# Attention with a spectral mixer on one core: instructions re-ordered within each engine by a table of moves

## The chip, the cores and the metric

One core of one Trainium2 chip runs the kernel: a matrix engine (TensorE, PE in the rows, its weight loads listed apart as PEld), VectorE (DVE), ScalarE (ACT), GpSimd (POOL), and SyncE (SP), whose queue issues nearly all transfers. The metric is device time in microseconds (us) of one launch. A profile of one execution gives the start, the length and the releasing event of each instruction.

## What is computed

Eight batches, each with eight heads of 576 positions and 64 channels. First attention with a threshold: of each score row only the entries within `tau` of the maximum are kept. Then a mixing layer over the 512 channels of a batch.

```
scores = (q @ k^T) / 8
scores = where(scores >= max(scores) - tau, scores, -1e9)
attn = exp(scores - max); attn = attn / (sum(attn) + 1e-9)
x = heads side by side of attn @ v             # per batch 576 x 512
theta = x @ w_theta
y = w_tok_r @ (x * cos(theta)) + w_tok_i @ (x * sin(theta))
u = x + y
out = u + max(u @ w_ch, 0)
```

## The kernel before

**Work.** Two heads make a pair; there are 32 pairs, four to a batch. A pair has five *units* of query rows, four with two heads of 128 rows and a last one in which both heads share 128 rows. Every fp32 operand of a product is split into a high and a low part (`xh` and `xl`, `q1` and `q2`, `k1` and `k2`), and three of the four cross products are taken.

**A unit.** Scores (L594: 12 matmuls of 288 columns, 6 in the last unit) go into the PSUM banks 0 to 3. VectorE reads each head's scores with its row maximum (L610) and so frees the banks; ScalarE takes the exponential (L635); VectorE masks and sums (L642). The weights are then turned round: in pairs 0 to 4 and in every fourth pair by TensorE (L675, copied out by ScalarE at L681 and L693), in the other 20 pairs by VectorE (L657, L659).

**A pair's end.** The product with v is L740 in the first kind of pair (72 matmuls in one run) and L711 in the second, where it works on 32-row by 64-column parts of the matrix engine; an L711 product comes in three blocks of 48 program matmuls (96 in the trace, since fp32 takes two passes), which the planner may place apart. The row sums are inverted by VectorE (L760, L764), transposed by TensorE (L768), sent through DRAM and multiplied into x by GpSimd (L791) or VectorE (L797).

**A batch's mixer.** Theta products and, at the end, w_ch products (both L843, 96 matmuls of 288 columns each), sines and cosines on ScalarE, transposes of z (L970) whose high and low parts are ScalarE's L976 and VectorE's L979, and 216 token matmuls (L999). The mixer of batch b runs between the pairs of batch b+1; the last batch's runs alone at the end. At the start the mixer's weights are split too (`convert`, L440 to L502).

**Order.** Nothing is ordered by hand. Every operation is recorded with a `key`, a due time built from the offsets in `AT`; `Plan.run` goes through a modelled execution, on each engine takes the ready operation with the lowest key, and then emits all instructions in order of their planned starts. Engines run their own lists in order and wait for each other by semaphores. PE's list is the one the rest hangs on. TensorE's instructions are counted in `supply`, in blocks of 256.

Of the kernel before, what the change touches and what calls it, by code (L numbers as in the profile page):

```python
# [10 lines left out]
F32 = mybir.dt.float32  # L11
# [18 lines left out]
BLOCK = 256  # L30
FETCH = 3.6
# [4 lines left out]
    "wait": 0.095, "margin": 46.124, "held": 12.206, "theta": 2.0, "theta_by": 8.31, "tok": 13.85, "tok_by": 3.19, "ch": 37.95,  # L36
    "ch_by": 9.28, "q": -2.78, "k": -4.2, "raw": 1.32, "v": 5.53, "m0": 8.11, "m1": 8.41, "score": -169.95, "nm": -1.15,
    "add": 0.82, "exp": -1.46, "mask": 2.68, "wrap": -18.89, "turn": 4.88, "copy": 2.04, "block": -0.74, "turn_by": -34.35,
    "last": 6.86, "v0": 2.89, "v1": 3.55, "vcopy": 9.91, "div": -3.88, "rows": 6.2, "dmul": 15.26, "x": -12.78, "x_by": 4.06,
# [3 lines left out]
    "n_rb": 2, "n_ang": 2, "n_xh": 4, "n_xl": 4, "n_wm": 3, "n_z": 3, "n_k": 4, "n_s2": 3, "n_nm": 4, "n_sc": 4, "n_a": 1,  # L43
    "n_zh4": 4, "n_zl4": 4, "n_zh1": 2, "n_zl1": 2, "n_xT": 7, "n_v": 1, "n_rows": 2, "n_rt": 1, "keep": -144.9,
    "linger": 0.174, "v_r": 1.74, "v_m": -2.19, "t_s": 1.07, "m_s": -9.19, "wc": 14, "early": 5, "each": 1, "ka": 4, "vq": 1,
    "pd": 3, "vs": 8.05, "parts": 3, "ab": 0, "sq": 2,
}

# [9 lines left out]
def BY_PE(n):  # L58
    return n < AT["early"] or n % 4 >= 4 - AT["each"]


def ON_POOL(what, n, j):
    if what == "q":
        return n >= 32 - AT["pq"]
    if what == "k":
        return j < AT["pk"]
    if what == "x":
        return j < AT["px"]
    if what == "u":
        return j < AT["pu"]  # L70
    return n < AT["pz"]
# [51 lines left out]
class Plan:  # L123
# [39 lines left out]
    def run(self):  # L163
        free = [0.7] * 5
        cand = [[] for _ in range(5)]
# [8 lines left out]
        block = [80, 0.0]  # L174

        def supply(o, t, occ):
            left, (at, ready), x = o.count, block, t
            while at + left >= BLOCK:
                x, left, at = max(x + (BLOCK - at) * occ / o.count, ready), left - BLOCK + at, 0
                ready = x + FETCH  # L180
            return x + left * occ / max(o.count, 1) - t - occ, [at + left, ready]
# [55 lines left out]
        while todo:  # L237
# [37 lines left out]
            for d in o.after:  # L275
                d.ready = max(d.ready, o.end + SEM if d.deps[o] else t)
# [5 lines left out]
        self.ops.sort(key=lambda o: (o.start, o.n))  # L282
        for o in self.ops:
            o.fn()
# [3 lines left out]
def tile_attn_moe(  # L288
# [36 lines left out]
    nc.sync.dma_start(tau_sb, tau.broadcast_to([P, 1]))  # L325
# [86 lines left out]
    wt_b = fixed(wt_h)  # L412

    def convert(src, n, raw_cls, places, key, done, turn):
# [125 lines left out]

    def prepare_q(n, key):
        pr = pairs[n]
        raw = sb("rawq", [P, QS])
        load(lambda: nc.sync.dma_start(raw(), qT[n // NP, n % NP]), key + AT["raw"], (), (raw,), 320)
        q1, q2 = pr.q = [sb("q", [P, QS], F32R) for _ in range(2)]
        if n >= AT["sq"]:
            act(
                c_act(QS, ptr=True), lambda: nc.scalar.activation(out=raw(), in_=raw(), func=AF.Copy, scale=gate), key,
                (raw,), (raw,),
            )  # L550
        act(c_act(QS), lambda: nc.scalar.copy(out=q1(), in_=raw()), key, (raw,), (q1,))
        low(ON_POOL("q", n, 0), lambda: q2(), lambda: raw(), lambda: q1().bitcast(F32), key, (raw, q1), (q2, 0), QS)

    def prepare_k(n, key):
        pr = pairs[n]
        raw = sb("rawk", [P, S])
        load(lambda: nc.sync.dma_start(raw(), kT[n // NP, n % NP]), key + AT["raw"], (), (raw,), 288)
        k1, k2 = pr.k = [sb("k", [P, S], F32R) for _ in range(2)]
        act(c_act(S), lambda: nc.scalar.copy(out=k1(), in_=raw()), key, (raw,), (k1,))  # L559
        low(ON_POOL("k", n, 0), lambda: k2(), lambda: raw(), lambda: k1().bitcast(F32), key, (raw, k1), (k2, 0))  # L560

    def load_v(n, key):
# [3 lines left out]

        def issue():
# [594 lines left out]
```

## Time and profile before

| | |
|---|---|
| time, three runs | 965.24, 966.85, 967.28 us; median 966.85 us |
| the profiled execution | 966.37 us, of which 964.6 us lie between its first and last instruction |
| PE busy | 914.9 us, 95% of the span |
| DVE, ACT, POOL busy | 816.2, 612.4, 353.4 us |
| granted TensorE clock | 1.00 (2.4 GHz) in every slice |

A busy PE is not PE at its peak: a matmul's end is modelled, about 0.3 us after its start, while the next one starts 0.13 us after it in a full run. A wait on PE therefore shows as idle time only beyond that.

### The profile page before, as it was taken

What the parts mean: (1) busy time and instruction counts of PE and PEld (TensorE: products, weight loads), DVE (VectorE), ACT (ScalarE), POOL (GpSimd) and SP (SyncE); (2) the same over time, 40 slices, a digit from 0 to 9 for tenths busy, and PEclk for the clock granted to TensorE, in tenths of its full rate; (3) what the DMA queues carried; (4) which work ended last, traced back from release to release, by engine and by line L of the source; (5) the groups of instructions that cost most, each with busy time, mean ns of one, the idle gap of its engine ahead of it and who ended that gap; (6) DMA issues with size and microseconds to landing.
All of it is one profiled execution on the core that took longest, in us unless ns stands there. A gap on an engine that the chain in (4) does not pass through costs nothing.

```text
span 964.6 us, 30108 instructions
## 1 busy us (share of the span) xinstructions
PE 914.9 (95%) x12532; PEld 804.4 (83%) x12532; DVE 816.2 (85%) x1981; ACT 612.4 (63%) x1156; POOL 353.4 (37%) x378
## 2 busy tenths in 40 slices
PE   5899899999999999999999999999999999999998
PEld 4567788897889889888898888888898878898898
DVE  6999989979899798879898798888898798985452
ACT  6889898447764667447874667637774467634550
POOL 4337635304362233522553242612443244510210
PEclk9999999999999999999999999999999999999999
DMA  7458244536613464325533365224633354123402
GB/s 236 124 157 252 64 126 140 144 120 188 176 53 83 127 188 119 90 65 162 182 79 96 99 201 142 69 61 143 187 98 90 100 170 150 47 56 106 158 8 72
DMA packets 60152, 118.81 MB, mean 123 GB/s; under 512 B 20560, under 2 KB 29296, under 8 KB 57456
## 3 DMA queue, kind: packets, MB, share of 16 engines
q1 hardware_dynamic: 60016, 116.90, 41.4%
q8 instruction: 98, 1.61, 0.7%
q14 instruction: 38, 0.31, 0.1%
HBM read 103.09 MB, written 13.78 MB: 121 GB/s over the span
## 4 chain that ended last, share of the span: by engine, by line
PE 52%; DVE 34%; ACT 7%; issue 4%; DMA 1%; POOL 1%; SPq 0%; DVEq 0%; ACTq 0%
PE banks_ps__66 L999 14%; PE banks_ps__66 L843 10%; PE banks_ps__66 L711 9%; DVE s L642 8%; DVE sc L610 8%; PE banks_ps__66 L594 8%; DVE a L657 6%; PE banks_ps__66 L675 4%; PE banks_ps__66 L740 3%; DVE zl L979 2%; DVE nm L619 1%; PE banks_ps__66 L970 1%; ACT s L635 1%; DVE z L895 1%; DVE xl L402 1%
## 5 line engine op out<-in xcount | busy, mean ns | idle before, releaser
L635 ACT ACTIVATE s<-sc,nm 128x576 f32<-128x576 f32 x288 | 218.2, 778 | 116.8 <-DVE sc L610 107.8
L642 DVE SCALAR_TENSOR_TENSOR s<-sc,nm,s 128x576 f32<-128x576 f32 x288 | 255.1, 900 | 7.2 <-ACT s L635 5.3
L610 DVE TENSOR_SCALAR_CACHE_REDUCE sc<-banks_ps__66 128x576 f32<-128x576 f32 x270 | 195.6, 739 | 18.1 <-PE banks_ps__66 L594 17.9
L594 PE MATMUL banks_ps__66<-k,q 64*128 64x288 f32 (+1 forms) x1728 | 176.8, 312 | 19.1 <-DVE sc L610 10.2
L594 PEld LDWEIGHTS banks_ps__66<-k,q 64*128 64x128 f32 (+1 forms) x1728 | 138.6, 188 | 48.1 <-DVE sc L610 19.5
L843 PE MATMUL banks_ps__66<-xh,wm 128*128 128x288 f32 x1024 | 173.2, 303 | 0.4 <-ACT xh L804 0.4
L999 PE MATMUL banks_ps__66<-wt_h,zh 128*128 128x288 f32 x576 | 159.5, 300 | 1.1 <-DVE zl L979 1.1
L999 PE MATMUL banks_ps__66<-wt_l,zh 128*128 128x288 f32 x576 | 159.8, 300 | 0.0
L843 PEld LDWEIGHTS banks_ps__66<-xh,wm 128*128 128x128 f32 x1024 | 143.8, 188 | 11.6 <-issue 9.2
L945 POOL TENSOR_TENSOR z<-z,xT 128x288 f32<-128x288 f32 x112 | 95.2, 886 | 143.3 <-ACT z L926 143.3
L657 DVE STREAM_TRANSPOSE a<-s 128x576 f32<-128x576 f32 x160 | 116.4, 756 | 14.5 <-PE banks_ps__66 L711 11.2
L791 POOL TENSOR_TENSOR xT<-xT,rb 128x288 f32<-128x288 f32 x48 | 38.4, 819 | 226.1 <-ACT xT L724 122.5
L711 PE MATMUL banks_ps__66<-a,v 32*64 32x144 f32 x5760 | 110.0, 287 | 5.5 <-issue 5.5
L999 PEld LDWEIGHTS banks_ps__66<-wt_h,zh 128*128 128x128 f32 x576 | 108.2, 188 | 4.4 <-issue 2.8
L999 PEld LDWEIGHTS banks_ps__66<-wt_l,zh 128*128 128x128 f32 x576 | 108.2, 188 | 4.0 <-issue 3.7
L711 PEld LDWEIGHTS banks_ps__66<-a,v 32*64 32x64 f32 x5760 | 91.8, 130 | 17.9 <-issue 17.1
L402 POOL TENSOR_TENSOR k<-rawk,k 128x288 fp32r<-128x288 f32 x64 | 64.7, 1031 | 107.2 <-ACT k L559 70.3
L999 PE MATMUL banks_ps__66<-wt_h,zl 128*128 128x288 f32 x576 | 96.0, 301 | 0.0
L843 PE MATMUL banks_ps__66<-xl,wm 128*128 128x288 f32 x512 | 94.5, 301 | 0.0
L402 POOL TENSOR_TENSOR xl<-xT,xh 128x288 fp32r<-128x288 f32 x64 | 62.5, 1003 | 71.5 <-ACT xh L804 70.1
L999 PEld LDWEIGHTS banks_ps__66<-wt_h,zl 128*128 128x128 f32 x576 | 81.0, 188 | 5.1 <-issue 5.0
L979 DVE TENSOR_TENSOR zl<-banks_ps__66,zh 128x512 fp32r<-128x512 f32 (+1 forms) x96 | 50.0, 544 | 34.0 <-ACT zh L976 33.3
(81 smaller groups left out, 1314.6 us busy)
## 6 DMA issues: line engine op xcount, KB each, us to landing
wm<-wm_dram SPq DMA_DIRECT2D x64, 512.0 KB
v<-in_vp_dram SPq DMA_DIRECT2D x104, 288.0 KB
rawq<-in_qT_dram SPq DMA_DIRECT2D x32, 320.0 KB
rawk<-in_kT_dram SPq DMA_DIRECT2D x32, 288.0 KB
out_dram<-xT SPq DMA_DIRECT2D x31, 288.0 KB
rb<-sums_dram SPq DMA_DIRECT2D x64, 128.0 KB
z<-in_w_tok_dram SPq DMA_DIRECT2D x9, 576.0 KB
wm_dram<-rb SPq DMA_DIRECT2D x16, 256.0 KB
```

The costliest lines, as they stand in the source:

```text
L402: eng.tensor_tensor(out=out()[:, c0:c1], in0=in0()[:, c0:c1], in1=in1()[:, c0:c1], op=ALU.subtract)
L594: nc.tensor.matmul(ps()[:, 2 * j + h, :HS], q[a]()[r, i * P : (i + 1) * P], k[c]()[r, h * HS : (h + 1) * HS], start=(x == 0), stop=(x == 2),)
L610: lambda j=j, sc=sc, scaled=scaled: nc.vector.tensor_scalar(out=sc().rearrange("p (a b) -> p a b", a=2), in0=ps()[:, 2 * j : 2 * j + 2, :H ...
L635: lambda j=j, sc=sc, weights=weights: nc.scalar.activation(out=weights(), in_=keys(sc()), func=AF.Exp, bias=nm()[:, j : j + 1], scale=-1.0),
L642: lambda j=j, sc=sc, total=total, weights=weights: nc.vector.scalar_tensor_tensor(out=weights(), in0=keys(sc()), scalar=nm()[:, 2 + j : 3 ...
L657: nc.vector.transpose(out=a()[:, :, j, 32 * i : 32 * i + 32], in_=src.rearrange("p (c q) -> p c q", q=32))
L675: nc.tensor.transpose(out=tp()[: k1 - k0, c * P : (c + 1) * P], in_=flat()[:, k0:k1], identity=ident)
L711: nc.tensor.matmul(ps()[64 * h : 64 * h + 64, b, :w], v()[r, c, h, :], a()[r, c, h, :], start=(c == 0), stop=(c == 17))
L843: nc.tensor.matmul(ps[h]()[:, :HS], wm()[:, a, c, :], parts[c][bb]()[:, h * HS : (h + 1) * HS], start=first and n == 0, stop=final and n = ...
L945: eng.tensor_tensor(out=zi, in0=zi, in1=x[m]()[:, c0:c1], op=ALU.mult)
L979: lambda zh=zh, zl=zl, tv=tv: nc.vector.tensor_tensor(out=zl(), in0=tv(), in1=zh().bitcast(F32), op=ALU.subtract),
L999: nc.tensor.matmul(ps()[:, :HS], zz[c][lo]()[:, zz[c][2]], w[:, c, hs], start=(q + n == 0), stop=(q + n == len(work) - 1),)
```

## The change

Five things are changed; the arithmetic of the result is the same, and each line issues as many matmuls as before.

1. The offsets in `AT` are new, with extra offsets for pairs 0 to 7 (`h_`) and from pair 28 on (`e_`); the planner adds a latency (`pad_`) to a dependence on another engine, and models TensorE's instruction blocks with a lead of `AHEAD` instructions.
2. After the planned order is made, a table `MOVES` with a list of steps for each engine moves single operations forwards or backwards on their engine; `settled` then emits all of them in an order that keeps the dependences.
3. Pair 0's q and k are loaded and split in two pieces each, and VectorE takes their low parts and one copy; `tau` comes through ScalarE's queue.
4. v is stored in DRAM as often as its rows are needed, and one transfer replaces two or four.
5. Small ones: the clamp of the weights on GpSimd has its two limits the other way round; the low part of `u` of the third chunk is GpSimd's from batch 1 on (`pu` 3); pair 2's scores are scaled when read, as those of pairs 0 and 1 (`sq` 3).

```diff
-FETCH = 3.6
+AHEAD = 61
...
-    "fa": -2.57, "fa_by": -1.76, "ft": -0.2, "ft_by": -5.1, "pq": 28, "px": 2, "pu": 2, "pz": 7, "pk": 1, "ta": 4, "cut": 2,
...
+    "linger": 0.14, "v_r": 1.69, "v_m": -0.73, "t_s": -0.29, "m_s": 8.46, "wc": 14, "early": 5, "late": 8, "fetch": 3.667,
+    "pad_pe": 0.12, "pad_dve": 0.021, "pad_act": 0.148, "rc": 0, "za": 0, "zq": 0, "ab0": 0, "rc0": 0, "za0": 0, "zq0": 0,
...
+MOVES = (
+    (
+        "0*7 1 -1 0*3 1 -1 0 0 1 1 -2 0 1 -1 0*18 3 -1*3 0*6 2 -1 -1 0*3 1 -1 0*3 1 -1 0 2 0 -2 0 0 1 -1 0*6 1 -1 1 "
...
+def A(what, n):
+    return AT[what] + AT["h_" + what] if n < 8 else AT[what] + AT["e_" + what] if n >= 28 else AT[what]
...
-                d.ready = max(d.ready, o.end + SEM if d.deps[o] else t)
+                d.ready = max(d.ready, o.end + SEM + pads[d.eng] * (d.eng != e) if d.deps[o] else t)
...
+    def settled(self):
+        lines = []
+        for e, moves in enumerate(MOVES):
+            line = [o for o in self.ops if o.eng == e]
+            steps = [int(w.split("*")[0]) for w in moves.split() for _ in range(int((w + "*1").split("*")[1]))]
+            final = [None] * len(line)
+            for i, (o, step) in enumerate(zip(line, steps, strict=True)):
+                final[i + step] = o
+            lines.append(final[::-1])
...
-    nc.sync.dma_start(tau_sb, tau.broadcast_to([P, 1]))
+    nc.scalar.dma_start(tau_sb, tau.broadcast_to([P, 1]))
...
-                out=mb().bitcast(F32)[:, r], in0=mb().bitcast(F32)[:, r], scalar1=W_LEAST, scalar2=W_MOST, op0=ALU.max, op1=ALU.min
+                out=mb().bitcast(F32)[:, r], in0=mb().bitcast(F32)[:, r], scalar1=W_MOST, scalar2=W_LEAST, op0=ALU.min, op1=ALU.max
...
+    def pieces_q(n):
+        return ((0, P), (P, QS)) if n == 0 else ((0, QS),)
+
+    def pieces_k(n):
+        return ((0, HS), (HS, S)) if n == 0 else ((0, S),)
...
+            if n == 0 and i == 0:
+                dve(c_fast(w), lambda r=r: nc.vector.tensor_copy(out=q1()[:, r], in_=raw()[:, r]), k, ((raw, i),), ((q1, i),), lock=True)
...
-            src = vp[n // NP, n % NP].rearrange("(r f) -> r f", r=rows)
-            for r in range(0, P, rows):
-                nc.sync.dma_start(v()[r : r + rows].rearrange("p c h d -> p (c h d)"), src)
...
+            src = vp[n // NP, n % NP, : P * each].rearrange("(p f) -> p f", p=P)
+            nc.sync.dma_start(v().rearrange("p c h d -> p (c h d)"), src)
```

**Three places in the built order.** The table of moves tells a reader nothing; these rows do. First the start of VectorE's list. L402 takes a low part, L610 reads scores; in the changed kernel these are L562 and L805, and L729 is the new copy of q. Before:

```order
L334 TENSOR_SCALAR small<-small 128x1
L335 TENSOR_SCALAR small<-small 128x1
L336 TENSOR_TENSOR small<-small 128x1
L402 TENSOR_TENSOR q<-rawq,q 128x640
L610 TENSOR_SCALAR sc,nm<-banks_ps__66,small 128x576 x2
```

and now:

```order
L729 CAST q<-rawq 128x128
L562 TENSOR_TENSOR k<-rawk,k 128x288
L562 TENSOR_TENSOR q<-rawq,q 128x128
L562 TENSOR_TENSOR k<-rawk,k 128x288
L576 TENSOR_SCALAR small<-small 128x1
L577 TENSOR_SCALAR small<-small 128x1
L578 TENSOR_TENSOR small<-small 128x1
L562 TENSOR_TENSOR q<-rawq,q 128x512
L805 TENSOR_SCALAR sc,nm<-banks_ps__66,small 128x576 x2
```

The low parts of pair 0 stand on VectorE in four small steps before the first read of scores; before, k's were GpSimd's and q's one step.

Second, TensorE at the v product of pair 22, in the middle of the program. `a,v` is a block of that product (L711, now L906), `zh` and `zl` are token matmuls (L999, now L1224), `xh,wm` is a w_ch matmul, `ident,rows` the transpose of the row sums. Before:

```order
L711 MATMUL banks_ps__66<-a,v 64x144 x48
L999 MATMUL banks_ps__66<-wt_l,zh_9407 128x288
L999 MATMUL banks_ps__66<-wt_h,zh_9407 128x288
L999 MATMUL banks_ps__66<-wt_l,zh_9407 128x288
L999 MATMUL banks_ps__66<-wt_h,zl_9409 128x288 x4
L999 MATMUL banks_ps__66<-wt_h,zl_9273 128x288
L999 MATMUL banks_ps__66<-wt_h,zl_9412 128x288 x4
L711 MATMUL banks_ps__66<-a,v 64x144 x48
L843 MATMUL banks_ps__66<-xh,wm 128x288 x12
L711 MATMUL banks_ps__66<-a,v 64x144 x48
```

and now:

```order
L1224 MATMUL banks_ps__66<-wt_h,zl_9352 128x288 x4
L1224 MATMUL banks_ps__66<-wt_h,zl_9276 128x288
L1224 MATMUL banks_ps__66<-wt_h,zl_9354 128x288
L906 MATMUL banks_ps__66<-a,v 64x144 x96
L961 MATMUL banks_ps__66<-ident,rows 9x128
L1036 MATMUL banks_ps__66<-xh,wm 128x288 x12
L1224 MATMUL banks_ps__66<-wt_h,zl_9354 128x288 x3
L906 MATMUL banks_ps__66<-a,v 64x144 x48
```

Two of the three blocks now follow each other, and the transpose of the row sums, which stood ten rows ahead of the first block, stands behind them.

Third, TensorE at the end: the last v product (`a,v` x36, L740, now L935), after which only the last batch's mixer is left. Before:

```order
L740 MATMUL banks_ps__66<-a,v 64x288 x36
L843 MATMUL banks_ps__66<-xh,wm 128x288 x4
L843 MATMUL banks_ps__66<-xl,wm 128x288 x4
L843 MATMUL banks_ps__66<-xh,wm 128x288 x8
L843 MATMUL banks_ps__66<-xl,wm 128x288 x4
L843 MATMUL banks_ps__66<-xh,wm 128x288 x8
L843 MATMUL banks_ps__66<-xl,wm 128x288 x4
L843 MATMUL banks_ps__66<-xh,wm 128x288 x8
L843 MATMUL banks_ps__66<-xl,wm 128x288 x4
L843 MATMUL banks_ps__66<-xh,wm 128x288 x20
```

and now:

```order
L1036 MATMUL banks_ps__66<-xl,wm 128x288 x8
L935 MATMUL banks_ps__66<-a,v 64x288 x36
L1036 MATMUL banks_ps__66<-xh,wm 128x288 x12
L1036 MATMUL banks_ps__66<-xl,wm 128x288 x6
L1036 MATMUL banks_ps__66<-xh,wm 128x288 x6
L1036 MATMUL banks_ps__66<-xl,wm 128x288
L1036 MATMUL banks_ps__66<-xh,wm 128x288 x2
L1036 MATMUL banks_ps__66<-xl,wm 128x288
```

The last 40 w_ch matmuls of batch 6 stood behind this v product and now stand before it; what follows it is theta of batch 7, first 18 matmuls on the three other pairs' x.

## Rows read from the trace of the kernel before

**Rows 1.** Page, part 1: busy time, share of the span, instructions of each engine.

```profile
PE 914.9 (95%) x12532; PEld 804.4 (83%) x12532; DVE 816.2 (85%) x1981; ACT 612.4 (63%) x1156; POOL 353.4 (37%) x378
```

**Rows 2.** Windows: busy us of PE, PEld, DVE, ACT, POOL, clock, DMA.

```profile
0.00:120.00 120.00, 98.66 (x841) 74.77 (x841) 109.52 (x270) 101.53 (x214) 62.12 (x59) 1.00 0.54 167
120.00:900.00 780.00, 757.40 (x11250) 671.89 (x11249) 678.89 (x1662) 486.68 (x900) 284.73 (x313) 1.00 0.42 121
900.00:964.60 64.60, 58.86 (x443) 57.76 (x443) 27.79 (x49) 24.14 (x45) 6.57 (x8) 1.00 0.22 73
```

**Rows 3.** PE's waits, 120 to 900 us: total us, times, longest.

```profile
PE banks_ps__66 L768 <- DVE rows L764: 6.9, 11, 0.7
PE banks_ps__66 L594 <- DVE sc L610: 6.5, 9, 1.3
PE banks_ps__66 L711 <- issue: 5.5, 8, 1.4
```

**Rows 4.** Timeline at pair 8's transpose: start, length, engine, line; idle before and releaser.

```profile
246.02 1.23 PE L843 MATMUL banks_ps__66<-xh,wm 128*128 128x288 f32 x8
...
247.60 0.17 DVE L764 RECIPROCAL rows<-rows 128x9 f32<-128x9 f32 x1
...
247.91 0.27 PE L768 MATMUL banks_ps__66<-ident,rows 128*9 128x128 f32 x1 [0.66 <-DVE rows L764]
```

**Rows 5.** Timeline behind pair 8's last unit.

```profile
235.98 1.16 PE L843 MATMUL banks_ps__66<-xh,wm 128*128 128x288 f32 x6
...
237.39 0.75 DVE L610 TENSOR_SCALAR_CACHE_REDUCE sc<-banks_ps__66 128x576 f32<-128x576 f32 x1
...
238.20 1.06 PE L594 MATMUL banks_ps__66<-k,q 64*128 64x288 f32 x12 [1.06 <-DVE sc L610]
```

**Rows 6.** Timeline: two blocks of the v product of pair 30.

```profile
867.97 1.36 PE L999 MATMUL banks_ps__66<-wt_h,zl 128*128 128x288 f32 x9
...
869.25 1.78 PE L711 MATMUL banks_ps__66<-a,v 32*64 32x144 f32 x96
...
870.96 0.67 PE L843 MATMUL banks_ps__66<-xh,wm 128*128 128x288 f32 x3
...
871.56 1.20 PE L711 MATMUL banks_ps__66<-a,v 32*64 32x144 f32 x53
...
873.35 0.99 PE L711 MATMUL banks_ps__66<-a,v 32*64 32x144 f32 x43 [0.59 <-issue]
```

**Rows 7.** Timeline: the one place with two blocks in a row.

```profile
421.04 3.16 PE L711 MATMUL banks_ps__66<-a,v 32*64 32x144 f32 x182
...
425.38 0.48 PE L711 MATMUL banks_ps__66<-a,v 32*64 32x144 f32 x10 [1.17 <-issue]
```

**Rows 8.** Page, part 3: a DMA queue, its packets, MB, share of 16 engines.

```profile
q8 instruction: 98, 1.61, 0.7%
```

**Rows 9.** Timeline: the first 9 us.

```profile
0.74 0.40 SPq L325 DMA_DIRECT2D small<-in_tau_dram  x1
...
4.82 0.67 ACT L559 CAST k<-rawk 128x576 fp32r<-128x576 f32 x1 [2.49 <-DMA rawk<-in_kT_dram]
...
6.38 1.42 DVE L402 TENSOR_TENSOR q<-rawq,q 128x640 fp32r<-128x640 f32 x1 [2.19 <-ACT q L551]
...
6.41 2.30 PE L594 MATMUL banks_ps__66<-k,q 64*128 64x288 f32 x12 [6.41 <-ACT q L551]
...
8.74 0.82 DVE L610 TENSOR_SCALAR_CACHE_REDUCE sc<-banks_ps__66,small 128x576 f32<-128x576 f32 x1 [0.94 <-PE banks_ps__66 L594]
```

**Rows 10.** Timeline: behind the last v product.

```profile
894.33 1.58 POOL L791 TENSOR_TENSOR xT<-xT,rb 128x288 f32<-128x288 f32 x2 [17.70 <-DMA rb<-sums_dram]
...
898.56 2.40 ACT L804 CAST xh<-xT 128x576 fp32r<-128x576 f32 x4 [4.32 <-PE banks_ps__66 L843]
...
916.60 1.29 PE L970 MATMUL banks_ps__66<-ident,z 128*128 128x128 f32 x9 [1.92 <-DVE zl L979]
```

**Rows 11.** Groups by line: mean ns of one | idle before.

```profile
L402 POOL TENSOR_TENSOR xl<-xT,xh 128x288 fp32r<-128x288 f32 x64 | 62.5, 1003 | 71.5 <-ACT xh L804 70.1 <-issue 1.4
```

More of the change, by code (lines that the diff above doesn't have):

```diff
@@ L35 @@
 AT = {
[L36 to L39, printed above, removed]
[3 rows of a table removed]
@@ L43 @@
[L43 to L46, printed above, removed]
-}
+    "h_add": -1.27, "e_add": 0.38, "h_block": 4.8, "e_block": 5.1, "h_ch": -9.02, "e_ch": 3.22, "h_ch_by": 8.82,
@@ L58, in BY_PE, with OF @@
 def BY_PE(n):
-    return n < AT["early"] or n % 4 >= 4 - AT["each"]
+    k = AT["late"]
+    return n < AT["early"] or (n + 1) * k // 32 > n * k // 32
+def A(what, n):
+    return AT[what] + AT["h_" + what] if n < 8 else AT[what] + AT["e_" + what] if n >= 28 else AT[what]
+def OF(what, b):
+    return AT[what + "0" if b == 0 else what]
 def ON_POOL(what, n, j):
@@ L66, in ON_POOL @@
         return j < AT["pk"]
[L67 to L70, printed above, removed]
+    if what in "xu":
+        return j < OF("p" + what, n)
     return n < AT["pz"]
@@ L172, in run @@
         todo = len(self.ops)
-        block = [80, 0.0]
+        stock = [80, 0.0, 0.0]
         def supply(o, t, occ):
[L177 to L181, printed above, removed]
+            if not o.count:
+                return 0.0, stock
+            (at, now, then), left, x, per = stock, o.count, t, occ / o.count
+            while left > 0:
+                goal = BLOCK - AHEAD if at < BLOCK - AHEAD else BLOCK
+                if at + left < goal:
+                    at, x, left = at + left, x + left * per, 0
+                    break
+                x, left, at = x + (goal - at) * per, left - (goal - at), goal
+                if goal < BLOCK:
+                    then = max(x, now) + AT["fetch"]
+                else:
+                    x, at, now = max(x, now), 0, then
+            return x - t - occ, [at, now, then]
         def begin(o):
@@ L282, in run @@
         self.ops.sort(key=lambda o: (o.start, o.n))
-        for o in self.ops:
-            o.fn()
+        for o in self.settled() if MOVES else self.ops:
+            o.fn()
+    def settled(self):
[7 more added lines that the diff above has]
+            lines.append(final[::-1])
+        before, users, owner = {o: set(o.deps) for o in self.ops}, {}, {}
+        for o in self.ops:
+            for b in o.bufs:
+                users.setdefault(b, []).append(o)
+        seen = set()
+        for o in self.ops:
+            for b in (*o.bufs, *o.hold):
+                if b.cls is None or b in seen:
+                    continue
+                seen.add(b)
+                for place in range(b.slot, b.slot + b.wide):
+                    old = owner.get((b.cls, place))
+                    owner[b.cls, place] = b
+                    for user in users[b] if old else ():
+                        before[user].update(u for u in users[old] if u is not user)
+        out, done = [], set()
+        while any(lines):
+            ready = [line for line in lines if line and before[line[-1]] <= done]
+            line = min(ready, key=lambda x: x[-1].start)
+            out.append(line.pop())
+            done.add(out[-1])
+        return out
 @with_exitstack
@@ L916, in sines @@
             work = [(zs[m], i) for m in ms for i in range(2)]
[L917 removed]
+            k, before = now() + A("sin", NP * b + NP), None
             for z, i in work:
@@ L1134 @@
                     qz[b, p, d, c : c + w] = qh[b, p, d, 512 + w * e : 512 + w * (e + 1)]
-            vv[b, p] = v[b, 2 * p : 2 * p + 2].reshape(2, S // rows, rows, D).transpose(2, 1, 0, 3).reshape(-1)
+            once = v[b, 2 * p : 2 * p + 2].reshape(2, S // rows, rows, D).transpose(2, 1, 0, 3).reshape(-1)
+            vv[b, p, : runs * once.size] = _np.tile(once, runs)
     wr = _np.asarray(inputs["moe_w_tok_r"]).T
```

226 lines of the change are left out of this document (157 added, 69 removed), and 95 rows, old and new, of tables (AT, MOVES).

## The prediction

> **What bounds the kernel now.** First the share of busy time: PE is busy for 95% of the span and no other engine for more than 85% [rows 1]. Then the same by stage [rows 2]. Up to 120 us PE has 98.7 us of work in 120 and VectorE 109.5: the start is VectorE's, which splits weights and handles pairs 0 to 4 at once. From 120 to 900 us PE has 757.4 of 780 and VectorE 678.9: PE bounds, 22.6 us are idle. In the last 64.6 us only the last mixer is left, PE at 58.9. The clock is 1.00, the upper level, throughout, so nothing is to be had from it. Both kernels have the same 9,196 program matmuls. The change can therefore only move the 22 us that PE misses at the start, the 23 in the middle and the 6 at the end, and what PE loses when it changes between kinds of matmul.
>
> Then the chain of waits for PE in the middle [rows 3]. Three kinds make 18.9 of the 22.6 us: the transpose of the row sums waits for VectorE's reciprocal (6.9 us, 11 times), scores wait until VectorE has read the unit before (6.5, 9 times), and the v product L711 stops with nothing to wait for, "issue" (5.5, 8 times).
>
> **Row sums.** At pair 8 the last matmul ahead of L768 starts at about 246.94 (eight from 246.02, 0.131 us apart), the reciprocal ends at 247.77, and L768 starts at 247.91 instead of 247.07 [rows 4]: 0.84 us lost, of which 0.66 show as idle, since a busy PE is shown to 0.3 us after its last start. So the 11 waits lose 6.9 + 11 x 0.17 = 8.8 us. Counted in the order, with 0.131 for a matmul of 288 columns [rows 4], 1.2 for a unit of scores and 0.7 for a VectorE pass over 576 columns, PE has 10.4 us of work between pair 8's last scores and L768, and VectorE 9.1 from reading them to the reciprocal: 1.3 us more on PE, and it waits. All pairs that wait have 0.9 to 1.3; none with 1.6 or more does. In the changed order, of the 24 pairs from 8 on one has 1.2, one 1.5, all others 1.7 to 7; pair 22 in the second place shown is such a one. Two waits of 0.8 stay: **-7.2 us**; since VectorE's order moved too, I take -6.5 (bounds 0 and -8.8).
>
> **Scores.** Banks 0 to 3 hold one unit's scores. After a pair's last unit only six matmuls (0.8 us) stand ahead of the next scores in every fourth pair, and PE waits 1.06 us for L610, which VectorE begins at 237.39 [rows 5]. Six of the 9 waits are these. The new order puts 28 matmuls there in pair 8, six in pair 12 as before, nine in the others: 0.4 us more cover each, all of it in pair 8. 4 x 0.4 + 1.1 is 2.7: **-2.5 us** (bounds +2 and -6.5; the wait could also return elsewhere).
>
> **Blocks of the v product.** L711 works on parts of the array, and entering it and leaving it costs. In the rows from 867.97 to 871.56, nine matmuls, one block and three matmuls take 3.59 us [rows 6]; at 0.131 and at 18 ns a block matmul (96 from 869.25 to 870.96) they would take 1.57 + 1.71 = 3.28. The 0.31 holds two entries and one exit, about 0.1 each, so 0.17 to 0.2 goes with a block. The 60 blocks stand in 59 runs before; now 16 pairs of them are joined and there are 44 runs. 15 x 0.17 = **-2.6 us** (bounds -2 and -4).
>
> **What joining costs.** PE's instructions come in blocks: 98 packets of 16.4 KB [rows 8] for 12,532 matmuls and as many loads [rows 1], so 256 in each. Counted in the built order, the eight stops of [rows 3] stand whole multiples of 256 instructions apart, at one place in the block, each inside an L711 product. There 256 instructions (128 matmuls at 18 ns) are used up in 2.3 us, faster than the next arrive. The only joined block of before stops for 1.17 us after 182 of its 192 matmuls [rows 7], a single one for 0.59 [rows 6]. A stop loses its idle time plus 0.26 (the shown end runs 0.28 past the start, 0.02 later the next would start): 5.5 + 8 x 0.26 = 7.6 us in all, 1.43 for the full one. In the changed order, if the boundaries fall at the same count, nine come after 256 instructions of nothing, or nearly nothing, but L711 (before: one, and seven with 2.6 to 2.8 us of work), and one more after 2.75 us. 9 x 1.3 + 0.95 = 12.6: **+5.0 us** (bounds -3, ten stops of half that of before, and +13, ten of the longest of before, 1.4 + 0.26, and four partial ones).
>
> The Trainium skill ("Runtime: NRT & Kernel Launch", section "Instruction fetch mechanics") says of this that a stream is refilled in 16 KiB blocks of 256 instructions and that crossing a boundary is mostly hidden. The block size agrees with the row; that it is hidden does not, with 5.5 us in 8 stops. By the page the joining would cost nothing, the term would be 0 and the sum 950.5.
>
> **Start.** PE's first scores wait for q until 6.41, VectorE spends 6.38 to 7.80 on q's low part, and only at 8.74 does it read the first scores [rows 9]. Now k comes in halves and q's first 128 columns alone, one 0.4 us issue earlier, since `tau` left the queue [rows 9]; the first scores need both halves of k (as many bytes as before) but not all of q, so k's second half can be cast at about 4.8, where all of k is cast today, and PE starts at about 5.0. VectorE then does k's low parts (0.45 each), q's first, the three small steps and the rest of q's low part (0.6 us) ahead of L805: about 7.0 instead of 8.74. VectorE is the bound of this stage, so **-1.7 us** (bounds 0 and -2.3), and -1.0 more for other waits of the 21.3 idle us there that a better order may save (0 to -4).
>
> **End.** Before, all x parts of the last batch are cast at 898.56 to 900.96, after the old w_ch matmuls; then PE misses 1.92 us at 916.60 and about 1.5 ahead of the first transposes of z [rows 10]. Now 40 w_ch matmuls leave the place behind the last v product, so the other three x parts are ready earlier; 18 matmuls (2.4 us) cover the last one, which needs the copies (0.9 us), L791 (1.58 [rows 10]) and a cast (0.6), 3.3 us with the waits between: PE waits about 1.0 there. The z transposes are now mixed with 12 theta matmuls and three of token (2 us). 1.0 for 3.4, with 0.4 left over: **-2.0** (bounds +2 and -3.5).
>
> **At nothing.** v: no wait of PE in [rows 3] is for a transfer, and the next v has a whole pair, some 27 us, to land; the cover gone, a transfer's 2 to 4 us. `pu` 3: seven low parts go from VectorE to two GpSimd steps of 1.0 us [rows 11], a whole token group (54 matmuls, 7 us) ahead of their use; GpSimd has 285 of 780 us [rows 2]. `sq`, the clamp: off PE's path in a stage bound by VectorE; below 0.7 us either way.
>
> **Sum.** -6.5 - 2.5 - 2.6 + 5.0 - 1.7 - 1.0 - 2.0 = -11.3 us on the profiled execution's 966.37 (964.6 of span and 1.8 around it): 955.1. The median of the runs is 966.85, half a microsecond above: **955.5 us**.
>
> **Rivals.**
> (a) The waits only move. VectorE's order changed wherever PE's did; if half of the row-sum and score terms return as waits for masks or casts, and the end gains nothing, -11.3 + 4.5 + 2.0 leaves -4.8: 962. For it: VectorE is at 87% in the middle and has little room [rows 2]. Against: the margins counted for L768 grew in nearly all pairs.
> (b) Joining costs nothing, because the boundaries fall elsewhere or the blocks come sooner: term 0, 950.5; with every stop gone, -7.6, it would be 943. For it: [rows 3] has only 8 stops for 59 runs. Against: all stand at the same count, and the one joined block stopped. The Trainium skill's page on the runtime, named above, would have it so.
> (c) Slower: the joined blocks stop for much longer, since refills share the engines with transfers. To end at 969 the term must be +18 instead of +5, 26 us over ten boundaries, 2.6 each; the longest stop today is 1.4 idle, 1.7 lost [rows 3]. It decides from there.
> (d) No effect within what a measurement tells: (a) and a term of +9 for the stops together.
>
> **Chances.** Main sum 0.58, (a) 0.17, (b) 0.10, (c) 0.08, (d) 0.07. The main case's own range is 950 to 960. Range 944 to 967: it leaves out (c), the far end of (b) and a part of (d). A change of 0.2% is about what can be told from none here: 964.9 and 968.8. Faster 0.82 (main, (a), (b), less 0.03), same 0.09, slower 0.09.
>
> **What would show it.** After: PE's wait for the reciprocals below 2 us and 4 times; scores' wait near 4; "issue" at the v product near 10 us in ten or so stops, each after a joined block; first scores at about 5.0 and their first read near 7.0; one wait of about 1 us behind the last v product. The prediction is wrong if "issue" does not grow, or if PE's wait for VectorE returns under another line.

## The result and the profile after

The changed kernel takes 957.13 us (median of 4 runs, 954.42 to 960.36) against 967.07 us (4 runs) for the kernel before: a ratio of 0.9898, 95% interval 0.986 to 0.9935. The forecast was 955.5 us. The profiled execution took 957.68 us, with a span of 955.9. One of the twelve executions of a later run, clamp_back, took 1005.56 us at a granted clock of 0.849 and is left out of what is said of that run.

The first part of the page and the windows of the changed kernel answer to [rows 1, 2]; columns as there.

```profile
PE 909.6 (95%) x12532; PEld 806.1 (84%) x12532; DVE 825.2 (86%) x1978; ACT 608.8 (64%) x1156; POOL 342.0 (36%) x390
```

```profile
0.00:120.00 120.00, 104.59 (x898) 80.50 (x899) 112.48 (x285) 106.45 (x226) 44.21 (x60) 0.99 0.52 165
120.00:900.00 780.00, 754.15 (x11252) 675.50 (x11252) 690.08 (x1651) 482.20 (x896) 293.07 (x325) 1.00 0.37 122
900.00:955.90 55.90, 50.90 (x386) 50.08 (x384) 22.61 (x44) 20.20 (x35) 4.72 (x6) 1.00 0.21 74
```

In the first 120 us TensorE now does 104.6 us of work in place of 98.7, and GpSimd has 44.2 us in place of 62.1. In the middle TensorE is idle for 25.9 us, more than the 22.6 of before. Its waits there, after, stand against [rows 3] (L906 is the v product, L784 the scores, L961 the transposed row sums, L1036 the theta and w_ch products):

```profile
PE banks_ps__66 L906 <- issue: 12.6, 9, 2.3
PE banks_ps__66 L784 <- DVE sc L805: 3.7, 7, 0.9
PE banks_ps__66 L1036 <- issue: 2.5, 3, 1.5
PE banks_ps__66 L961 <- DVE rows L957: 1.5, 2, 0.8
PE banks_ps__66 L784 <- issue: 1.2, 1, 1.2
```

The row sums' wait went from 6.9 to 1.5 us and the scores' from 6.5 to 3.7, but the stops with no releaser grew from 5.5 us in 8 to 16.3 in 13. The stop also shows on the line that comes next when a joined block ends at it (L1036, L784). Counted by 256 along TensorE's instructions in the trace, 12 of the 13 stand at one place (remainder 193 to 196), as the eight of before do (194 to 196), and hold 15.8 us; the 13th, 0.46 us at 891.58, is no such stop but a wait behind the last v product. The timeline of the changed kernel, TensorE and VectorE, at the places that the next paragraphs use:

```profile
4.61 2.11 PE L784 MATMUL banks_ps__66<-k,q 64*128 64x288 f32 x12 [4.61 <-ACT k L745]
...
7.16 0.81 DVE L805 TENSOR_SCALAR_CACHE_REDUCE sc<-banks_ps__66,small 128x576 f32<-128x576 f32 x1
...
213.34 0.40 PE L784 MATMUL banks_ps__66<-k,q 64*128 64x288 f32 x2
...
248.33 3.25 PE L906 MATMUL banks_ps__66<-a,v 32*64 32x144 f32 x192
...
499.81 2.95 PE L906 MATMUL banks_ps__66<-a,v 32*64 32x144 f32 x171
505.06 0.71 PE L906 MATMUL banks_ps__66<-a,v 32*64 32x144 f32 x21 [2.31 <-issue]
...
886.52 4.59 PE L935 MATMUL banks_ps__66<-a,v 64*64 64x288 f32 x72
891.58 2.15 PE L1036 MATMUL banks_ps__66<-xh,wm 128*128 128x288 f32 x12 [0.46 <-issue]
...
904.80 0.77 PE L1179 MATMUL banks_ps__66<-ident,z 128*128 128x128 f32 x5 [1.47 <-DVE z L1154]
```

The same two marks in the timeline of the kernel before, the first scores of pair 8 and the last v product:

```profile
218.00 0.40 PE L594 MATMUL banks_ps__66<-k,q 64*128 64x288 f32 x2
...
888.79 4.60 PE L740 MATMUL banks_ps__66<-a,v 64*64 64x288 f32 x72
```

They cut the span in three. **Start:** pair 8 begins 4.7 us earlier, and by then 28 more theta and w_ch matmuls (0.131 us each) and 5 more transposes (about 0.11) are done, counted by kind in both traces, 4.2 us of work: **-8.9**. **Middle:** from there to the last v product it is 673.2 us against 670.8, with 16 more matmuls and 5 fewer transposes in it (1.6 us): **+0.8**. **End:** from there 69.4 against 75.8, with 44 fewer matmuls (5.8 us): **-0.6**. The sum is -8.7, the difference of the spans.

So the total came near the forecast and the stages did not: all that the middle gained went into stops, and into two drops of TensorE's clock right behind two of them, 3.4 us, which the last section shows.

### The profile page after: what moved, and what is told of

Same layout as the page of the kernel before. It is cut to its first block, busy times and chain, and to the rows that moved or that the text cites. A ratio compares the mean times of both kernels' runs of the same rounds, so it can differ in the third digit from the quotient of the medians.

```text
span 955.9 us, 30042 instructions
## 1 busy us (share of the span) xinstructions
PE 909.6 (95%) x12532; PEld 806.1 (84%) x12532; DVE 825.2 (86%) x1978; ACT 608.8 (64%) x1156; POOL 342.0 (36%) x390
## 4 chain that ended last, share of the span: by engine, by line
PE 62%; DVE 23%; ACT 7%; issue 5%; DMA 1%; POOL 1%; SPq 0%; DVEq 0%; POOLq 0%; ACTq 0%
PE banks_ps__66 L1224 20%; PE banks_ps__66 L1036 12%; PE banks_ps__66 L784 10%; PE banks_ps__66 L906 9%; DVE sc L805 6%; DVE s L837 6%; PE banks_ps__66 L870 4%; DVE a L852 4%; PE banks_ps__66 L1179 3%; PE banks_ps__66 L935 2%; ACT s L830 1%; DVE nm L814 1%; DVE xl L562 1%; DVE zl L1204 1%; ACT xh L997 1%
## 5 line engine op out<-in xcount | busy, mean ns | idle before, releaser
L837 DVE SCALAR_TENSOR_TENSOR s<-sc,nm,s 128x576 f32<-128x576 f32 x288 | 249.5, 886 | 9.1 <-ACT s L830 6.5
L805 DVE TENSOR_SCALAR_CACHE_REDUCE sc<-banks_ps__66 128x576 f32<-128x576 f32 x261 | 188.4, 744 | 16.4 <-PE banks_ps__66 L784 15.2
L784 PE MATMUL banks_ps__66<-k,q 64*128 64x288 f32 (+1 forms) x1728 | 176.9, 315 | 15.3 <-DVE sc L805 8.5
L784 PEld LDWEIGHTS banks_ps__66<-k,q 64*128 64x128 f32 (+1 forms) x1728 | 139.3, 190 | 44.8 <-DVE sc L805 16.4
L1036 PE MATMUL banks_ps__66<-xh,wm 128*128 128x288 f32 x1024 | 170.5, 303 | 3.1 <-issue 2.5
L1224 PE MATMUL banks_ps__66<-wt_l,zh 128*128 128x288 f32 x576 | 160.4, 301 | 0.0
L1224 PE MATMUL banks_ps__66<-wt_h,zh 128*128 128x288 f32 x576 | 159.4, 302 | 0.0
L1036 PEld LDWEIGHTS banks_ps__66<-xh,wm 128*128 128x128 f32 x1024 | 143.9, 189 | 9.9 <-issue 7.2
L852 DVE STREAM_TRANSPOSE a<-s 128x576 f32<-128x576 f32 x160 | 117.6, 758 | 14.4 <-PE banks_ps__66 L906 13.3
L562 POOL TENSOR_TENSOR xl<-xT,xh 128x288 fp32r<-128x288 f32 x78 | 75.6, 991 | 124.1 <-ACT xh L997 93.9
L906 PE MATMUL banks_ps__66<-a,v 32*64 32x144 f32 x5760 | 105.4, 286 | 13.2 <-issue 12.6
L562 POOL TENSOR_TENSOR k<-rawk,k 128x288 fp32r<-128x288 f32 x62 | 59.1, 959 | 150.1 <-ACT k L745 148.7
L906 PEld LDWEIGHTS banks_ps__66<-a,v 32*64 32x64 f32 x5760 | 91.1, 130 | 23.4 <-issue 19.9
L1224 PEld LDWEIGHTS banks_ps__66<-wt_h,zh 128*128 128x128 f32 x576 | 107.2, 188 | 4.1 <-issue 3.0
L1224 PEld LDWEIGHTS banks_ps__66<-wt_l,zh 128*128 128x128 f32 x576 | 108.0, 189 | 3.0 <-issue 2.9
L1224 PE MATMUL banks_ps__66<-wt_h,zl 128*128 128x288 f32 x576 | 98.6, 301 | 0.0
L1036 PE MATMUL banks_ps__66<-xl,wm 128*128 128x288 f32 x512 | 93.1, 301 | 0.8 <-POOL xl L562 0.8
L1224 PEld LDWEIGHTS banks_ps__66<-wt_h,zl 128*128 128x128 f32 x576 | 83.1, 190 | 2.4 <-issue 2.3
L562 POOL TENSOR_TENSOR q<-rawq,q 128x320 fp32r<-128x320 f32 x56 | 56.8, 1026 | 66.2 <-ACT q L731 64.4
L876 ACT COPY a<-banks_ps__66 128x128 f32<-128x128 f32 (+1 forms) x144 | 65.4, 488 | 22.8 <-PE banks_ps__66 L870 22.4
```

Of the source, the lines that this page charges most:

```text
L562: eng.tensor_tensor(out=out()[:, c0:c1], in0=in0()[:, c0:c1], in1=in1()[:, c0:c1], op=ALU.subtract)
L784: nc.tensor.matmul(ps()[:, 2 * j + h, :HS], q[a]()[r, i * P : (i + 1) * P], k[c]()[r, h * HS : (h + 1) * HS], start=(x == 0), stop=(x == 2),)
L805: lambda j=j, sc=sc, scaled=scaled: nc.vector.tensor_scalar(out=sc().rearrange("p (a b) -> p a b", a=2), in0=ps()[:, 2 * j : 2 * j + 2, :H ...
L837: lambda j=j, sc=sc, total=total, weights=weights: nc.vector.scalar_tensor_tensor(out=weights(), in0=keys(sc()), scalar=nm()[:, 2 + j : 3 ...
L852: nc.vector.transpose(out=a()[:, :, j, 32 * i : 32 * i + 32], in_=src.rearrange("p (c q) -> p c q", q=32))
L876: lambda c0=c0, nb=nb, tp=tp: nc.scalar.copy(out=a()[:, c0 : c0 + nb, e, q0 : q0 + P], in_=tp()[:, : nb * P].rearrange("p (c q) -> p c q", ...
```

## Experiments

Theory A: a stop belongs to a place in TensorE's instruction stream, counted by 256, and lasts as long as the work ahead is too short to cover the next block's arrival. Theory B: it belongs to the joined v products or to transfers beside them. A second question was what made the start so much shorter.

| run | median us | ratio to before, 95% | stops 120 to 900 us: idle, times |
|---|---|---|---|
| changed kernel | 957.13 | 0.9898 (0.986 to 0.9935) | 16.3, 13 |
| phase_46 | 948.86 | 0.9815 (0.9796 to 0.9833) | 6.3, 7 |
| phase_22 | 954.64 | 0.9881 (0.9859 to 0.9903) | 13.1, 13 |
| phase_64 | 960.45 | 0.9921 (0.9898 to 0.9944) | 16.1, 13 |
| before_phase | 960.72 | 0.994 (0.9921 to 0.9959) | 0.2, 1 |
| parted | 949.7 | 0.9818 (0.9802 to 0.9834) | 2.7, 4 |
| parted2 | 952.47 | 0.9844 (0.9823 to 0.9866) | 0.7, 2 |
| clamp_back | 964.27 | 0.9977 (0.9962 to 0.9992) | 16.5, 12 |
| before_clamp | 966.07 | 0.9996 (0.9981 to 1.0012) | 4.4, 6 |
| before_planned | 984.97 | 1.019 (1.0163 to 1.0217) | 6.4, 7 |
| no_moves | 973.92 | 1.009 (1.0067 to 1.0114) | 11.5, 13 |
| loads_whole | 959.42 | 0.9922 (0.9901 to 0.9943) | 16.2, 12 |
| v_four | 955.11 | 0.9883 (0.9871 to 0.9896) | 14.3, 12 |

The last column adds the rows "issue" of the waits, as above. In the changed kernel and the runs that stand on it, other than clamp_back and no_moves, about 0.46 us in one of the times is the wait behind the last v product.

**The place in the stream: phase_46, phase_22, phase_64.** Small matmuls run ahead, while TensorE has nothing to do, and shift the place of all that follows:

```diff
-    nc.vector.memset(magic, MAGIC)
+    nc.vector.memset(magic, MAGIC); [nc.tensor.matmul(psum[0:1, 7, 0:1], ident[:, 0:1], ident[:, 0:1], start=True, stop=True) for _ in range(46)]
```

> 46 one-column fp32 matmuls (184 instructions) run on TensorE into a bank not yet in use, while TensorE waits for its first operands; nothing else moves. Theory A, the stops belong to the place in TensorE's instruction stream: in the traces of before and after every long stop without a releaser stands at the same remainder when the instructions are counted by 256, and what a stop costs is near 3.75 us less the work of the 256 instructions ahead of it. By that count the changed kernel should lose 16.3 us in such stops (the trace has 16.3 with no releaser), and with all later instructions 184 places on, 9.8: 6 us fewer, so about 951 to 953 us, with 0 to 1 us given back at the start, and the blocks that stop are other ones. Theory B, a stop belongs to the joined v products themselves or to transfers that run beside them: the same blocks stop for the same time, 957 to 958 us.

> The same with 22 one-column matmuls (88 instructions). Theory A: by the same count 21.7 us are lost in stops in place of 16.3, with 12 in place of 8 blocks stopping inside a full v product: about 961 to 963 us. Theory B: 957 to 958 us, as with 46 and as without any.

> 64 one-column matmuls, 256 instructions, ahead of everything: the places of all later instructions counted by 256 are those of the changed kernel. It tells whether the 46 and the 22 of the earlier runs helped by where they put the later instructions or by being there. Theory A, only the place counts: the stops are back at the same blocks and at 18 to 21 us in sum, the time at 956 to 959 us, with 0 to 1 us for the longer row of small matmuls. Rival, early matmuls help by themselves: 948 to 952 us.

With 46 the stops fall from 16.3 to 6.3 us, and other blocks stop. In the timeline of phase_46 a joined block stops that ran through at 248.33 above, and the one which stopped for 2.31 us at 505.06 now runs through its 192 matmuls:

```profile
249.65 2.50 PE L906 MATMUL banks_ps__66<-a,v 32*64 32x144 f32 x142
253.59 1.14 PE L906 MATMUL banks_ps__66<-a,v 32*64 32x144 f32 x50 [1.45 <-issue]
...
499.59 3.25 PE L906 MATMUL banks_ps__66<-a,v 32*64 32x144 f32 x192
```

Pair 8 begins at 214.68 in phase_46, 1.3 us later than in the changed kernel, and from there to the last v product it is 661.0 us in place of 673.2: the gain lies where the stops were and not at the start. Of these 12.2 us 3.4 are the two drops of the clock, which do not occur there. With 64, a whole block of 256 instructions, the stops are back: 16.1 us in 13, nearly all at the same blocks. That is theory A, and theory B falls.

The trace also shows what TensorE waits for. Queue q8 of [rows 8] brings the blocks, one packet of 16.4 KB each. The packet that landed at 503.65 comes 1.41 us before the end of the stop at 505.06, and so it is with all of them: the eight stops of before and the 12 of the changed kernel end 1.3 to 1.6 us after a packet has landed, and all 115 stops at that place of the count, in the traces of before, after and the twelve experiments, 1.2 to 1.6 us after.

The sizes were only roughly right. With 46 the time came out 2 us below the expected range. With 22, 21.7 us were to go into stops and the trace has 13.1, less than the changed kernel, not more; the time was to rise by 5 us and is 2.5 us lower, within the intervals. phase_64 has the changed kernel's stops and a median 3.3 us above it, outside what was expected; its granted clock is lower. Its execution at 0.995 took 955.64 us and the five at 0.989 to 0.991 took 958.54 to 961.52; the changed kernel took 954.42 to 957.68 us at 0.993 to 0.995 and 960.36 at 0.989.

**The same in the kernel before: before_phase** (44 of the small matmuls).

> The kernel before with 44 one-column matmuls (176 instructions) ahead and nothing else. What is open: whether the stops of the kernel before, 7.6 us by the prediction's count, could have been had by their place alone, without any of the change. Theory A: counted by 256 its boundaries then fall where the instructions ahead hold 3.2 us of work or more in all places but one; the stops that the trace shows without a releaser go from 5.5 us in 8 to 1 us in one or two, and the run takes 960 to 962 us. Rival, as in the two runs with the parted products, other waits take the place of the stops: 964 to 967 us with the stops gone all the same.

Its waits answer to [rows 3]:

```profile
PE banks_ps__66 L768 <- DVE rows L764: 7.0, 11, 0.7
PE banks_ps__66 L594 <- DVE sc L610: 5.1, 10, 1.1
PE banks_ps__66 L711 <- issue: 0.2, 1, 0.2
```

The stops are gone, the row sums' wait is where it was, and the time is 5.9 us shorter in the same runs. Pair 8 begins where it did (218.02), and from there to the last v product it is 664.1 us in place of 670.8. Place alone was worth 6 us in the kernel before, more than half of what the whole change gave.

**Taking the stops apart: parted, parted2.** Both stand on phase_46. In TensorE's line single parts of v products change place, later in the first, mostly earlier in the second, so that other products stand in the stretch ahead of a boundary:

```diff
+LATER = ((220, 223), (345, 349), (403, 405), (397, 400), (589, 591), (584, 586), (947, 951), (1183, 1184), (1362, 1367))
...
-            lines.append(final[::-1])
+            [final.insert(after, final.pop(part)) for part, after in LATER if e == PE]; lines.append(final[::-1])
```

> The kernel with 46 one-column matmuls ahead, and nine parts of v products put back by two to five places in TensorE's line, so that 1.2 to 1.6 us of other products stand inside the stretches in which that run's trace shows its long stops (0.5 to 1.8 us each, 10.7 us in 14). Theory A, a stop is the part of a refill that the work of the instructions ahead doesn't cover: the stops go from 10.7 to about 4 us, parting costs 9 x 0.17 = 1.5 us, so 943 to 945 us against 948.9. Rival: the stops come with the v products wherever they stand, or the moved products make their readers wait as long: 948 to 951 us.

> As with the nine parted v products, but mostly the other way: six parts of v products stand earlier in TensorE's line, so that products which stood ahead of them fall between two parts, and two stand later (three moves in all are later or short). In the first form the scores came right behind a late part and waited 4.1 us for ScalarE's copies out of the banks that both use. Theory A: the stops fall from 10.7 to about 4 us and that wait stays near nothing: 944 to 946 us. Rival: a part put earlier waits for its own blocks, or the products put back hold up their readers, and the gain is lost again: 948 to 950 us.

The stops did go, to 2.7 and 0.7 us, and nothing was gained: 949.7 and 952.47 us against 948.86. In parted the scores, which share banks with the v product, stand right behind a late part and wait for ScalarE to copy it out; the waits and the timeline of parted:

```profile
PE banks_ps__66 L784 <- ACT xT L922: 4.1, 5, 0.8
```

```profile
254.07 1.78 PE L906 MATMUL banks_ps__66<-a,v 32*64 32x144 f32 x96
256.65 1.07 PE L784 MATMUL banks_ps__66<-k,q 64*128 64x288 f32 x12 [0.81 <-ACT xT L922]
```

In parted2 the parts wait for their own blocks, and one transpose until VectorE has added a token product that came late (L1236):

```profile
PE banks_ps__66 L784 <- DVE sc L805: 4.8, 8, 1.1
PE banks_ps__66 L870 <- DVE xT L1236: 3.0, 1, 3.0
...
PE banks_ps__66 L906 <- DVE a L854: 1.9, 3, 1.1
```

All rows of TensorE's waits from 120 to 900 us without the stops make 12.0 us in phase_46, 18.0 in parted and 19.2 in parted2: 6.0 and 7.2 us more, against 3.6 and 5.6 us of stops saved. phase_46 stays the fastest of all, 0.9815, though parted lies within its interval, and nothing was gained by taking more of its stops away.

**The clamp: clamp_back, before_clamp, before_planned.**

```diff
-                out=mb().bitcast(F32)[:, r], in0=mb().bitcast(F32)[:, r], scalar1=W_MOST, scalar2=W_LEAST, op0=ALU.min, op1=ALU.max
+                out=mb().bitcast(F32)[:, r], in0=mb().bitcast(F32)[:, r], scalar1=W_LEAST, scalar2=W_MOST, op0=ALU.max, op1=ALU.min
```

> The clamp of the weights' conversion takes its two bounds in the order of before (max with the lower one first, then min with the upper), all else as in the changed kernel. Theory A, the order of the two operations sets GpSimd's time: the 28 pieces take 37 us again in place of 16 us (1347 ns each in place of 593), the weights are converted later, and of the 8 us that the first eight pairs gained some 2 to 4 go: 959 to 962 us. Rival: the 28 pieces were shorter for another reason (who else used the memory), then they stay at 593 ns and the time at 957; or they are long again but off the path, then the time stays within 1 us of 957.

Undone in the changed kernel it costs 7.1 us. GpSimd's groups for the clamp in the changed kernel, and then in clamp_back (count | busy us, mean ns | idle before):

```profile
L613 POOL TENSOR_SCALAR xl<-xl 128x288 f32<-128x288 f32 (+1 forms) x28 | 16.2, 593 | 53.7 <-DVE xh L634 22.6 <-ACT xl L608 22.6 <-DVE nm L814 5.4
```

```profile
L613 POOL TENSOR_SCALAR xl<-xl 128x288 f32<-128x288 f32 (+1 forms) x28 | 36.0, 1300 | 45.7 <-DVE xh L634 20.4 <-ACT xl L608 18.5 <-DVE sc L805 4.5
```

The waits of clamp_back up to 126 us show the way to the path: VectorE, the bound there, stands behind GpSimd's pieces, and TensorE behind VectorE (in the changed kernel the first of these rows is missing, and the other two read 4.8 and 2.6).

```profile
DVE xh L627 <- POOL xl L613: 2.2, 4, 1.1
```

```profile
PE banks_ps__66 L784 <- DVE sc L805: 6.7, 7, 1.8
PE banks_ps__66 L870 <- DVE s L837: 5.3, 8, 2.0
```

Pair 8 starts at 221.09 in place of 213.34, 7.8 us later: the whole loss falls into the start. Some 1.7 us of it is clock (granted 0.97 up to 120 us in place of 0.99); the rest is the waits.

> The kernel before with one edit of the change alone: the clamp takes the upper bound with min first, then the lower one with max. Nothing is moved. With the clamp's order undone in the changed kernel its 28 pieces took GpSimd long again and the run 964.6 us in place of 957.1, so theory A: the edit by itself is worth most of what the whole change gave; GpSimd's 28 pieces take 16 us in place of 37 and the run 959 to 961 us. Rival: the kernel before was planned for slow pieces and its lines do not use the shorter ones, then 965 to 967 us; the price shows only in lines planned for it.

> The kernel before with the clamp's order turned, and with the planner's cost of a piece on GpSimd lowered by the same factor as in the change (1.7 to 0.7), so that the lines are planned for the short pieces. Counted by 256 the stops are worth about as much as before (9 against 9 us). Theory A, the shorter pieces are worth what the plan makes of them: the eighth pair, at 218.0 us before, begins 4 to 8 us earlier and the run takes 959 to 962 us. Rival: GpSimd's pieces are off the path of that kernel in any order, as the run with the turned order alone has it: 965 to 968 us, or some other time from the new plan as a whole with the eighth pair where it was.

In the kernel before, the same edit is worth nothing (0.9996), though its pieces shrink from 37.3 to 17.3 us. With the planner told of the shorter pieces the run is 18 us longer, far outside what was expected: the scores' wait for VectorE is 13.3 us over the span in place of 10.2, pair 8 begins at 223.1, and the granted clock of the profiled execution is 0.988, some 12 us of full speed lost where that of the kernel before lost none. Why its clock fell so often was not tested. So the edit is no gain by itself; the new lines depend on it. Theory A was wrong in both runs.

**The table: no_moves** (`MOVES = ()`).

> The changed kernel with the table of single moves emptied, so that each engine runs its line as the planner left it with the new numbers. Theory A, the table is where the shorter waits come from: the waits of the reciprocals, the scores and the weights come back, some 5 to 10 us, and by the count of instruction blocks the stops take 21.8 us in place of 16.3: 965 to 972 us. Rival, the planner's new numbers, the first pair's pieces and the clamp carry the gain and the moves are noise: 955 to 960 us.

973.92 us, 16.8 more than with the table and 2 above the expected range. The waits of no_moves from 120 to 900 us:

```profile
PE banks_ps__66 L784 <- DVE sc L805: 8.4, 15, 1.2
PE banks_ps__66 L961 <- DVE rows L957: 4.6, 10, 1.8
```

Pair 8 begins at 219.22, 5.9 us later than with the table. All the rest of the change without the table is slower than the kernel before; the moves are what shortens the scores' and the row sums' waits and a good part of the start. The stops are not where the table gains: 11.5 us without it. The moves of one engine by itself were not tried.

**The loads: loads_whole, v_four.**

```diff
-            load(lambda r=r: nc.sync.dma_start(raw()[:, r], qT[n // NP, n % NP][:, r]), k + A("raw", n), (), ((raw, i),), w // 2)
+            load(lambda r=r, i=i: i or nc.sync.dma_start(raw(), qT[n // NP, n % NP]), k + A("raw", n), (), ((raw, i),), w // 2)
```

(and k alike), and

```diff
-            nc.sync.dma_start(v().rearrange("p c h d -> p (c h d)"), src)
+            [nc.sync.dma_start(v()[r : r + rows].rearrange("p c h d -> p (c h d)"), src) for r in range(0, P, rows)]
```

with `src` one copy of v.

> The changed kernel with q and k of the first pair brought in whole, by the first of the two loads; the second load is empty, the pieces on the engines stay. Theory A, the pieces of the loads are what lets the first scores start at 4.6 us in place of 6.4: the first score matmul goes to 5.5 to 6.4 us and the end by as much, 958 to 959 us. Rival: the start has slack behind it (VectorE and the weights' conversion bound the first 120 us), then the first score matmul is later and the fifth pair and the end are where they were, within 1 us.

> The changed kernel with v brought in by two or four transfers of one copy, as before, in place of one transfer of all copies. Theory A, v's transfers are off the path: within 1 us of 957. Rival: the extra issues on SyncE's queue hold back what stands behind them, the row sums' transfers among them: 958.5 to 960 us; or the one long transfer was itself in the way: 954 to 956 us.

In the timeline of loads_whole the first scores and their first read are later by 1.9 and 1.3 us:

```profile
6.46 1.93 PE L784 MATMUL banks_ps__66<-k,q 64*128 64x288 f32 x12 [6.46 <-DVE q L729]
8.43 0.82 DVE L805 TENSOR_SCALAR_CACHE_REDUCE sc<-banks_ps__66,small 128x576 f32<-128x576 f32 x1 [0.26 <-PE banks_ps__66 L784]
```

Pair 5 begins 2.0 us later (116.9 against 114.9) and the run takes 2.3 us longer. But the intervals overlap, and the clock falls twice in this start, near 20 and 33 us, and once in the changed kernel's, which is 1.7 us by itself; the execution at 0.998 took 954.24 us. So the pieces bring the first scores forward, and what that is worth at the end is not shown. v in four transfers takes 955.11 us, 2.0 less, with overlapping intervals and in the range given for the rival that the one long transfer is in the way. No gain of the single transfer shows; whether it costs anything is open.

## Why the prediction was right, and by what luck

**Row sums: right.** -6.5 forecast; 5.4 us of idle and 9 waits fewer at 0.17 make -6.9. Two waits are left, as counted from the order.

**Scores: right.** -2.5 forecast, 6.5 to 3.7 is -2.8.

**What joining costs: mechanism right, size wrong.** The term was +5.0. By its own way of counting (idle plus 0.26 a stop) 7.6 us became 15.8 + 12 x 0.26 = 19.0, so +11.4, near the upper bound. The nine stops behind nothing but L711 came as counted, but cost 1.8 us each on average (0.87 to 2.31 idle) instead of 1.3; of others there were three instead of one. The price of a full stop was taken from the single one of before [rows 7]; the stops vary more than one row could show. Rival (c) named 2.6 us each as the point of no gain: the longest reached it, the mean did not. Rival (b), the boundaries falling elsewhere, was a matter of place: phase_46 is that case, and its 948.86 us lies 1.6 below the 950.5 given. The Trainium skill's sentence that a crossing is mostly hidden ("Runtime: NRT & Kernel Launch", section "Instruction fetch mechanics") agrees with the trace for all but 12 of the 98 blocks of the changed kernel; those 12, at v products, stop TensorE for 15.8 us. before_phase and phase_64 show both sides.

**The clock** was given as 1.00 throughout, "so nothing is to be had from it"; that the change could lose some of it had no term. Two drops in the middle, behind stops, cost 3.4 us and one in the start 1.7.

**Joining itself,** -2.6, was not measured alone. With the terms above and the two drops of the clock the middle comes to +2.5, and +0.8 was measured; the 1.7 us between them stay open. Whatever it saves, the stops cost more.

**Start: the step that failed.** The pieces of the first pair were right (scores at 4.61, read at 7.16; forecast 5.0 and 7.0). But -2.7 for the whole start was -8.9, because the clamp was put at nothing, "off PE's path in a stage bound by VectorE". VectorE was the bound, yet its list waited for GpSimd's pieces, so in the changed lines the clamp carries about 7 us, by clamp_back. The change itself gave the sign, in a line that the diff above leaves out: the planner's factor for such a piece went from 1.7 to 0.7.

**End:** -2.0 forecast, -0.6 measured. The wait behind the last v product is 0.46 us, less than the 1.0 forecast; but the first transposes of z wait 1.47 us, where 1.92 was to shrink to almost nothing [rows 10].

**At nothing:** that the single transfer of v gains nothing agrees with v_four; `pu` and `sq` were not tested. The sum was near by luck: a start under-sized by 6.2 us stood against stops under-sized by 6.4 us, 3.4 us of clock and an end 1.4 short.

## What to carry to other kernels

Count the instructions of the busiest engine by blocks before joining small matmuls: where a block is used up faster than the next one arrives, the place of the boundaries can be worth as much as the rest of a change (6 and 8 us here), and a few dozen small instructions at an idle start move it. A stop removed by hand in a tightly ordered line came back as waits on other lines in both tries here, so measure each. Look at the granted clock of every run before giving a difference of 2 us a cause. An operation on a lightly loaded engine is on the path as soon as the bounding engine's list waits for it.

## What was not expected of the hardware

**The order of two limits on GpSimd.** With max first a piece of 128x256 took 1.05 us before; with min first 0.38. The timelines of the kernel before and of the changed kernel, two pieces each:

```profile
8.25 2.09 POOL L445 TENSOR_SCALAR xl<-xl 128x256 f32<-128x256 f32 x2 [1.13 <-ACT xl L440]
```

```profile
10.80 0.76 POOL L613 TENSOR_SCALAR xl<-xl 128x256 f32<-128x256 f32 x2 [9.50 <-ACT xl L608]
```

Why is open; clamp_back, where nothing but the order differs, has the long pieces again.

**The granted clock.** In the profile of before it is 1.00 throughout. In the changed kernel it falls to the lower level (1.2 GHz) three times, near 70, 469 and 722 us. The windows of the first (TensorE's busy us, clock, DMA share, GB/s):

```profile
66.00:68.00 2.00, 0.58 (x5) 1.00 1.05 355
68.00:70.00 2.00, 1.39 (x15) 1.00 1.07 225
70.00:72.00 2.00, 2.00 (x9) 0.52 0.81 271
72.00:74.00 2.00, 2.00 (x11) 0.62 0.46 178
```

TensorE was idle for half of the 4 us before, waiting for VectorE's reads, and then ran near the lower level for a while: 0.48 x 2 + 0.38 x 2 = 1.7 us of full speed lost. The third comes right behind a long stop of a joined block:

```profile
721.30 0.46 PE L906 MATMUL banks_ps__66<-a,v 32*64 32x144 f32 x5 [2.28 <-issue]
```

```profile
718.00:720.00 2.00, 1.02 (x66) 1.00 0.56 213
720.00:722.00 2.00, 0.70 (x8) 1.00 0.01 2
722.00:724.00 2.00, 2.00 (x11) 0.51 0.03 8
724.00:726.00 2.00, 2.00 (x11) 0.64 0.00 0
```

That is 0.49 x 2 + 0.36 x 2 = 1.7 us again, and so is the second, behind the stop of 1.72 us that ends at 468.20: 5.1 us in all. Not every stop brings one: phase_46 has none behind its stops and phase_22, with stops of up to 1.9 us, none after 120 us. Times of one kernel go with the clock: the kernel before took 964.11 to 964.95 us at 1.000 and 965.31 to 968.48 at 0.996.

before_clamp shows 0.94 over its first 120 us, 7 us lost in the same way, with pair 5 at 124.8 us against 120.0 before. That is not why its shorter pieces gave nothing: its three executions at 1.000 took 963.0, 964.23 and 964.65 us, and four of the kernel before at that clock 964.11 to 964.95.
